# Reordering one seam of a gated-recurrence kernel: the third unit's scores, two output pieces, and ScalarE's copies of x

## The chip, the cores and the metric

The kernel runs on one core of a Trainium2 chip. Its time is the device time of one execution in microseconds (us); lower is better. The three runs of the kernel before gave 678.92, 680.96 and 681.97 us, so its median is 680.96 us.

## The reference

Two blocks follow each other. The first is a gated recurrence with a complex decay, over 4 batches, 8 heads, 768 positions and a head size of 48. Its output is read as 3072 tokens of width 384 and goes through a feed-forward block of width 2048 with an ELU.

```python
mag = sqrt(a_re**2 + a_im**2)
scale = minimum(mag, 0.999) / (mag + 1e-6)
a_re_n, a_im_n = a_re * scale, a_im * scale
for t in range(S):                       # S = 768
    S_re, S_im = (ar*S_re - ai*S_im + k_t v_t^T), (ar*S_im + ai*S_re)
    y[:, :, t] = q_t @ S_re
x = y.transpose(0, 2, 1, 3).reshape(B*S, H*D)
h = x @ w_in
g = where(h > 0, h, exp(minimum(h, 0)) - 1)
return g @ w_out
```

## The kernel before

**Units.** The work is cut into 12 units. A unit is 128 positions of two batches (so 256 tokens, GT), and the units of one pair of batches follow each other with a carried state. For every unit the kernel computes decays and angles (squares, logarithms, powers, lengths, ratios, slopes, angles, carried: ScalarE and VectorE), from them the gates (turns, waves, scaled, ends, gated), then on TensorE the transposes of the gated q and k, the scores, the products with v ("values") and with the carried states, and last the feed-forward block: eight times "inner" (two of 16 slices of w_in by x) with "elu" behind it, then the projection through w_out. TensorE is fed by every one of these.

**Order.** The program runs under a manual schedule: every engine and every DMA queue takes its instructions in the order in which the Python code emits them, and waits on semaphores that the tile framework puts in. For the first three units this order is a list written out by hand, `first` (L1429 to L1479); for the later ones it is a plan with slot numbers (L1489 to L1506). An entry such as `(project, 1, 0, 12, 16)` calls `project(u=1, n=0, f0=12, f1=16)`. The change lies in the last nine lines of this list, in which the projections of units 0 and 1 are spread as "pieces" between the steps of unit 2 (the third unit, `PAIRED` = 2) and the first steps of unit 3.

**A piece** is `project(u, n, f0, f1)` (L1205): four matmuls of 384 columns, written (u, n, f0, f1) below or, short, (u, n, f0). n is one half of the unit's tokens. The piece that ends at 16 also emits two ScalarE copies of 192 columns from PSUM to a tile `o` (L1224) and two output DMAs on SP's queue (L1225). The tag `o` has two buffers. The accumulators lie in PSUM: unit 0 has one bank of the tag `mlp` for each half; unit 1 has both halves in one tile of the tag `y`, which has one buffer:

```python
            if u == 0:
                x["o", n] = work([C, DM], "mlp")
            elif n == 0:
                t = ps.tile([C, NB, 512], FP32, tag="y", bufs=1, name="y")
                for m in range(NB):
                    x["o", m] = t[:, m, 0:DM]
```

PSUM's eight banks are three for `mlp`, three for `w` and two for `y`. `inner` (L1182) takes a bank of `mlp` for each call. When unit 2's inner begins, two of the three belong to the halves of unit 0's projection; the third was last used by `inner` (1, 14), whose elu comes much earlier in the list. Banks are given out in the order in which the program has given them back, so `inner` (2, 0) takes the third bank, (2, 2) that of the half n = 0 of unit 0 and (2, 4) that of n = 1; the later ones wait for the elus of these three.

**Around the third unit.** `states` (L1030) multiplies keys with values for the half 0 of unit 2. `transposed` (L1002) does eight TensorE transposes into two banks of `w`, and ScalarE copies each bank to SBUF (L1014). `scored` (L1116) does the state products of half 1 into two banks of `w` (L1054), then all scores into one tile `y` (L1126), and VectorE masks the two halves of it (L1134). `turns` of unit 3 is L832 on TensorE with four VectorE instructions behind it (L837, L840). `valued` (L1139) does the products with v into a new tile `y` (L1087), the sums of decays of unit 3 (`quartered`, L883), the products with the carried states (L1096), the exponentials of unit 3 on ScalarE (`quarters_used`, L898, and one DMA, L902), and last copies y to `x["x"]` and `x["y"]` on ScalarE (L1157, L1158). `seam` (L1162) moves rows of `x["y"]` to `x["x"]` by six DMAs, three on GpSimd's queue and three on SP's. `waves` of unit 3 is three ScalarE activations (L967, L970, L971). `convert` takes one step of rounding the weights, and does nothing once all of them are rounded: the list calls it 96 times for 80 steps, and the last step is taken before `(project, 1, 0, 4, 8)`.

Of the kernel before, what the change touches and what calls it, by code (L numbers as in the profile page):

```python
# [505 lines left out]
def kernel(  # L506
# [68 lines left out]
    nat = [{} for _ in range(NU)]  # L575
# [110 lines left out]
    def flat(t):  # L686
        return t.rearrange("p n h d -> p (n h d)")
# [5 lines left out]
    def new(tag, bufs=1, shape=None):  # L693
        return sb.tile(shape or [C, NB, H, D], FP32, tag=tag, bufs=bufs, name=tag)
# [182 lines left out]
    def quartered(u):  # L877

        x = nat[u]
        both = [work([C, HD]) for n in range(NB)]  # L880
        for c in range(C // L):
            for n, t in enumerate(both):
                nc.tensor.matmul(  # L883
                    t[ts(c ^ n, L)], lhsT=sum_logs[ts(c, L), ts(c, L)],
                    rhs=flat(x["l"][ts(c, L), n : n + 1]), start=True, stop=True,
                )
        return both

    def quarters_used(u, both):

        x = nat[u]
        for n, t in enumerate(both):
            for key, sign in (("E", 1.0), ("F", -1.0)):
                pairs = [(slice(0, C), slice(0, C))]
                if n:
                    pairs = [(ts(c, L), ts(1 - c, L)) for c in range(C // L)]
                for to, of in pairs:
                    nc.scalar.activation(  # L898
                        out=flat(x[key][to, n : n + 1]), in_=t[of], func=AF.Exp, scale=sign
                    )  # L900
        ends = dram.tile([NB, C // L, H, D], FP32, tag="ends", bufs=2, name="ends")
        nc.scalar.dma_start(  # L902
            out=ends.rearrange("n c h d -> c n (h d)"),
            in_=x["E"][L - 1 :: L].rearrange("p n h d -> p n (h d)"),
        )
        x["ends"] = ends
# [92 lines left out]
    PAIRED = 2  # L999
# [83 lines left out]
    def value_products(u, n, y, first=True):  # L1083
        x = nat[u]
        for p, c, j in EACH:

            nc.tensor.matmul(  # L1087
                y[ts(j, HP), c, ts(p, L)], lhsT=vn[u % 2][ts(c, L), n, ds((2 * p + j) * D, HP)],
                rhs=x["a", n][ts(c, L), 2 * p + j], start=(first and p == 0), stop=False,
                skip_group_check=True,  # L1090
            )
    def carried_products(u, n, y):
        x = nat[u]
        for p, c, j in EACH:
            if x["S", n][c] is not None:
                nc.tensor.matmul(  # L1096
                    y[ds(j * HP, D), c, ts(p, L)], lhsT=x["S", n][c][:, 2 * p + j],
                    rhs=x["qt", n][:, 2 * p + j, ts(c, L)], start=False, stop=False,
                    skip_group_check=True,
                )  # L1100
# [38 lines left out]
    def valued(u):  # L1139

        x = nat[u]
        y = ps.tile([C, C // L, 512], FP32, tag="y", bufs=1, name="y")
        for n in range(NB):
            value_products(u, n, y[:, :, ts(n, NP * L)], n == 0)
        if u + 1 < NU:
            both = quartered(u + 1)
        for n in range(NB):
            carried_products(u, n, y[:, :, ts(n, NP * L)])
        if u + 1 < NU:
            z = nat[u + 1]  # L1150
            z["E"], z["F"] = new("n", 6), new("n", 6)
            quarters_used(u + 1, both)
        x["x"], x["y"] = new("x", 2, [C, NI, GT]), new("y", 1, [C, GT])
        parts = y.rearrange("p c (n x t) -> p c n x t", n=NB, x=NP)
        to = x["x"].rearrange("p x (n c t) -> p c n x t", n=NB, c=C // L)
        for c in range(C // L):
            nc.scalar.copy(out=to[:, c], in_=parts[:, c, :, 0:NI])  # L1157
        nc.scalar.copy(  # L1158
            out=x["y"].rearrange("p (n c t) -> p c n t", n=NB, c=C // L), in_=parts[:, :, :, NI],
        )  # L1160
# [262 lines left out]
    def gates_of(u, *at):  # L1423
# [45 lines left out]
        *2 * [(convert,)], (project, 1, 1, 4, 8), (turns, 2), *2 * [(convert,)],  # L1469
        (project, 0, 1, 4, 8), (begun, 3), (squares, 3), *2 * [(convert,)],  # L1470
        (project, 1, 0, 8, 12), (waves, 2), (scaled, 2), (joined, 3), (gated, 2), (ends, 2),
        (load_qk, 3), (logarithms, 3), (powers, 3), (convert,), (project, 1, 1, 8, 12),
        *4 * [(convert,)], (states, 2, 0), *5 * [(convert,)], (project, 1, 0, 12, 16),
        (transposed, 2, "q", 0), (project, 1, 1, 12, 16), (transposed, 2, "k", 0), (lengths, 3),
        (ratios, 3), (slopes, 3), (transposed, 2, "q", 1), (angles, 3), (project, 0, 0, 8, 12),
        (transposed, 2, "k", 1), (carried, 3), (project, 0, 1, 8, 12), (scored, 2), (turns, 3),
        (project, 0, 0, 12, 16), (valued, 2), (seam, 2), (noted, 3), (waves, 3),
        (project, 0, 1, 12, 16), (scaled, 3), (ends, 3), (opened,),
    ]  # L1479
    def layer_of(u, at_h, at_p):  # L1480
        for m in range(NF // 2):
# [7 lines left out]
    for u in range(2, NU):  # L1489
        r = (u - 2) * SLOTS  # L1490
        put(r + (4 if u > PAIRED else 8), load_a, u)
        put(r + 8, load_v, u)
        put(r + 8, load_qk, u)
        if u == 2:
            decays_of(u, 16, 16, 17, 17, 18.4, 19.5, 19.6, 22.7, 19.8, 19.8)
            gates_of(u, 20.4, 21.6, 22.1, 22.4, 22.4, 22.6)
        else:
            decays_of(u, r + 7.2, r + 8.4, r + 12, r + 13.2, r + 13.4, r + 13.5, r + 14.9, r + 16.7, r + 15.5, r + 16.6)
            gates_of(u, r + 15, r + 18, r + 18.5, r + 18, r + 18, r + 19.5)
        if u > PAIRED:  # L1500
            for n in range(NB):
                put(r + 22 + 2 * n, transposed, u, "q", n)
                put(r + 23 + 2.3 * n, transposed, u, "k", n)
            put(r + 26.6, scored, u)
            put(r + (31 if u + 1 < NU else 29.3), valued, u)
            put(r + (31 if u + 1 < NU else 29.3), seam, u)  # L1506
        layer_of(u, range(r + 36, r + 44), range(r + 44, r + 52))
# [46 lines left out]
```

## Time and profile before

| | |
|---|---|
| median of three runs | 680.96 us |
| the profiled execution | 681.87 us |
| its span, first to last instruction | 680.1 us |
| TensorE busy (matmul) | 657.5 us, 97% |
| TensorE weight loads | 578.1 us, 85% |
| VectorE, ScalarE, GpSimd busy | 400.9, 395.9 and 184.2 us |
| granted TensorE clock, mean | 0.99 |
| the stage that the change reorders | 131.8 to 177.3 us of the span |

In the lists of the timeline a line gives the start in us, the duration, the engine (PE is TensorE, PEld its weight loads, DVE VectorE, ACT ScalarE, POOL GpSimd, SP the queue of SyncE), the line of the kernel, the operation, output and inputs with their shapes, the number of instructions, and in brackets how long the engine sat idle before it and what released it. Ends of matmuls are modelled, so two lines of PE may overlap by some tenths. One fp32 matmul of a piece shows as two instructions.

### The profile page before, as it was taken

Reading aid. Unit: us, or ns where it says so; the run is one execution under the profiler, and the core shown is the slowest. Engines: PE = TensorE matmul, PEld = TensorE weight load, DVE = VectorE, ACT = ScalarE, POOL = GpSimd, SP = SyncE. Lnnn points to the kernel's source line nnn. Section 1 sums busy time; section 2 is a strip of 40 time slices with the busy share of each in tenths; the row PEclk is TensorE's granted clock in tenths of the full one; section 3 lists DMA queues with packets and bytes.
Section 4 is the critical chain, followed back from the end, with each engine's and each line's share of the span. In section 5 each row is a group of like instructions: output and inputs, shape, how many; then the busy total and the mean of one; then the engine's idle time right before and its main releaser. Section 6 shows DMA issues by size and latency. Waiting matters only on the chain.

```text
span 680.1 us, 15754 instructions
## 1 busy us (share of the span) xinstructions
PE 657.5 (97%) x6656; PEld 578.1 (85%) x6656; DVE 400.9 (59%) x584; ACT 395.9 (58%) x620; POOL 184.2 (27%) x199
## 2 busy tenths in 40 slices
PE   8799898999999999999999999999999999999996
PEld 6777785566899899999999999999889889889995
DVE  5898999954775465465465465465564554642151
ACT  6875455875755755755756756657657557541230
POOL 2000000112114523433433433533434423501000
PEclk9799999999999999999999999999999999999999
DMA  9985744530902902812911821831821731200000
GB/s 169 187 141 93 146 144 167 109 71 20 166 12 68 149 26 66 140 37 62 142 39 54 134 54 54 134 56 54 125 64 53 137 53 52 50 2 7 24 1 29
DMA packets 149899, 55.98 MB, mean 82 GB/s; under 512 B 129172, under 2 KB 142652, under 8 KB 149820
## 3 DMA queue, kind: packets, MB, share of 16 engines
q1 hardware_dynamic: 146336, 53.57, 40.6%
q0 software_dynamic: 3264, 1.18, 1.7%
q8 instruction: 54, 0.88, 0.6%
q14 instruction: 25, 0.20, 0.1%
q10 hardware_dynamic: 220, 0.14, 0.1%
HBM read 48.88 MB, written 4.78 MB: 79 GB/s over the span
## 4 chain that ended last, share of the span: by engine, by line
PE 82%; DVE 9%; ACT 4%; issue 3%; DMA 1%; ACTq 0%; POOL 0%; DVEq 0%; POOLq 0%
PE mlp L1190 33%; PE mlp L1301 27%; PE w L1013 6%; PE y L1096 3%; PE y L1126 3%; PE w L1054 3%; PE y L1087 2%; PE w L832 2%; DVE wf L43 1%; DVE w_out L653 1%; DVE wp L50 1%; DVE g L1201 1%; PE mlp L1404 1%; PE y L1216 1%; PE w L883 1%
## 5 line engine op out<-in xcount | busy, mean ns | idle before, releaser
L1190 PE MATMUL mlp<-x,w_in 128*128 128x256 f32 x1152 | 262.6, 382 | 4.6 <-DVE g L1201 2.7
L1190 PEld LDWEIGHTS mlp<-x,w_in 128*128 128x128 f32 x1152 | 215.5, 191 | 34.8 <-DVE g L1201 3.1
L1199 ACT ACTIVATE ee<-mlp 128x512 f32<-128x512 f32 x96 | 57.3, 597 | 137.2 <-PE mlp L1190 128.3
L1201 DVE SCALAR_TENSOR_TENSOR g<-ee,mlp 128x512 f32<-128x512 f32 x96 | 65.6, 684 | 117.8 <-ACT ee L1200 107.9
L1301 PE MATMUL mlp<-w_out,g 128*128 128x192 f32 x640 | 110.3, 326 | 0.0
L1301 PEld LDWEIGHTS mlp<-w_out,g 128*128 128x128 f32 x640 | 105.5, 190 | 2.7
L1279 DVE TENSOR_TENSOR g<-g 128x512 f32<-128x512 f32 x80 | 67.4, 842 | 2.7
L1200 ACT ACTIVATE ee<-ee 128x512 f32<-128x512 f32 x96 | 60.5, 630 | 2.9
L1071 POOL TENSOR_TENSOR S<-S,T 128x384 f32<-128x384 f32 x36 | 29.9, 849 | 102.5 <-DVE S L1069 102.5
L1301 PE MATMUL mlp<-w,g 128*128 128x192 f32 x320 | 55.8, 329 | 0.0
L1301 PEld LDWEIGHTS mlp<-w,g 128*128 128x128 f32 x320 | 52.1, 190 | 0.6
L1170 POOL DMA_DIRECT2D x<-y x62 | 30.5, 498 | 75.1 <-ACT y L1158 38.0
L1320 ACT COPY o<-mlp 128x192 f32<-128x192 f32 x10 | 3.2, 319 | 67.8 <-DMA out_dram<-o 39.9
L898 ACT ACTIVATE n<-w 64x384 f32<-64x384 f32 (+1 forms) x60 | 28.1, 486 | 18.4 <-PE w L883 17.7
L993 POOL TENSOR_TENSOR kg<-k,cs 128x1536 f32<-128x1536 f32 x8 | 34.8, 4351 | 12.6 <-issue 12.5
L856 POOL DMA_DIRECT2D carry<-n x10 | 5.1, 505 | 120.0 <-DVE n L840 120.0
L716 POOL TENSOR_TENSOR n<-n 128x768 f32<-128x768 f32 x8 | 16.5, 2059 | 67.6 <-ACT n L710 67.6
L759 POOL TENSOR_TENSOR n<-ar,n 128x768 f32<-128x768 f32 x8 | 14.9, 1861 | 61.0 <-ACT n L747 61.0
L1301 PE MATMUL mlp<-wt,g 128*128 128x192 f32 x160 | 29.4, 327 | 0.0
L1013 PE MATMUL w<-ident,qg 128*128 128x128 f32 x192 | 26.3, 283 | 1.9 <-ACT kt L1014 1.2
L993 DVE TENSOR_TENSOR qg<-q,cs 128x1536 f32<-128x1536 f32 (+1 forms) x12 | 19.5, 1622 | 14.8 <-ACT cs L971 14.8
L821 DVE SCALAR_TENSOR_TENSOR n<-carry,n 1x768 f32<-1x768 f32 x10 | 9.5, 947 | 31.5 <-ACT n L815 31.5
(173 smaller groups left out, 1008.8 us busy)
## 6 DMA issues: line engine op xcount, KB each, us to landing
w<-in_moe_w_out_dram SPq DMA_DIRECT2D x8, 768.0 KB
g<-in_moe_w_in_dram SPq DMA_DIRECT2D x16, 384.0 KB
g<-in_moe_w_out_dram SPq DMA_DIRECT2D x16, 384.0 KB
w<-in_moe_w_in_dram SPq DMA_DIRECT2D x16, 288.0 KB
vn<-in_v_dram SPq DMA_DIRECT2D x24, 192.0 KB
out_dram<-o SPq DMA_DIRECT2D x48, 96.0 KB
ar<-in_a_re_dram SPq DMA_DIRECT2D x22, 192.0 KB
ai<-in_a_im_dram SPq DMA_DIRECT2D x22, 192.0 KB
```

What stands on the lines that cost most here:

```text
L898: nc.scalar.activation(out=flat(x[key][to, n : n + 1]), in_=t[of], func=AF.Exp, scale=sign)
L993: eng.tensor_tensor(out=to[:, :, :, 0:D], in0=each.unsqueeze(2).to_broadcast([C, step * H, 2, D]), in1=x["cs"][:, n * H : (n + step) * H], ...
L1013: nc.tensor.transpose(t[:, h], of, ident)
L1054: nc.tensor.matmul(to, lhsT=of, rhs=vn[u % 2][ts(c, L), n, ts(h, D)], start=True, stop=True,)
L1071: eng.tensor_tensor(out=new_s, in0=new_s, in1=wide, op=ALU.mult)
L1170: eng.dma_start(out=x["x"][ds(j * HP + D, G), i], in_=x["y"][ds(j * HP + i * G, G)])
L1190: nc.tensor.matmul(t[:, e], lhsT=w_in[:, i, ts(f + e, C)], rhs=x["x"][:, i], start=(i == 0), stop=(i == NI - 1),)
L1199: nc.scalar.activation(out=e, in_=t, func=AF.Relu, scale=-1.0)
L1200: nc.scalar.activation(out=e, in_=e, func=AF.Exp, scale=-1.0)
L1201: nc.vector.scalar_tensor_tensor(out=x["g", f // 8][:, f % 8 : f % 8 + 2], in0=e, scalar=-1.0, in1=t, op0=ALU.add, op1=ALU.max)
L1279: nc.vector.tensor_tensor(out=S_of(u, k, h), in0=a, in1=b, op=op)
L1301: nc.tensor.matmul(to, lhsT=a[:, m], rhs=b[:, m], start=(first and h == 0 and m == 0), stop=False, skip_group_check=True,)
```

## The change

In `valued`, the three copies of y become a function of their own, `copied`. For unit 2 it is called before the exponentials of unit 3, for the later units after them, as before. In the list, the calls of the last part are put in another order, and ten calls of `convert`, all of them empty, are taken out.

```diff
@@ def valued(u)
+        if u == PAIRED:
+            copied(u, y)
         if u + 1 < NU:
             z = nat[u + 1]
             z["E"], z["F"] = new("n", 6), new("n", 6)
             quarters_used(u + 1, both)
+        if u > PAIRED:
+            copied(u, y)
+
+    def copied(u, y):
+        x = nat[u]
         x["x"], x["y"] = new("x", 2, [C, NI, GT]), new("y", 1, [C, GT])
...
@@ first = [
-        (load_qk, 3), (logarithms, 3), (powers, 3), (convert,), (project, 1, 1, 8, 12),
-        *4 * [(convert,)], (states, 2, 0), *5 * [(convert,)], (project, 1, 0, 12, 16),
-        (transposed, 2, "q", 0), (project, 1, 1, 12, 16), (transposed, 2, "k", 0), (lengths, 3),
-        (ratios, 3), (slopes, 3), (transposed, 2, "q", 1), (angles, 3), (project, 0, 0, 8, 12),
-        (transposed, 2, "k", 1), (carried, 3), (project, 0, 1, 8, 12), (scored, 2), (turns, 3),
-        (project, 0, 0, 12, 16), (valued, 2), (seam, 2), (noted, 3), (waves, 3),
-        (project, 0, 1, 12, 16), (scaled, 3), (ends, 3), (opened,),
+        (load_qk, 3), (logarithms, 3), (powers, 3), (project, 1, 0, 12, 16),
+        (states, 2, 0), (project, 1, 1, 8, 12), (transposed, 2, "q", 0), (lengths, 3),
+        (ratios, 3), (project, 0, 0, 8, 12), (transposed, 2, "k", 0), (transposed, 2, "q", 1),
+        (slopes, 3), (angles, 3), (project, 1, 1, 12, 16), (transposed, 2, "k", 1),
+        (carried, 3), (scored, 2), (turns, 3), (project, 0, 1, 8, 12), (valued, 2), (seam, 2),
+        (noted, 3), (waves, 3), (project, 0, 0, 12, 16), (scaled, 3), (ends, 3),
+        (project, 0, 1, 12, 16), (opened,),
```

## The prediction, made before the run

> **What bounds the kernel now.** I read the page first: TensorE is busy for 97% of the span and is 82% of the chain that ended last, so only TensorE's gaps can be won, and any new gap is lost in full.
>
> ```profile
> span 680.1 us, 15754 instructions
> ...
> PE 657.5 (97%) x6656; PEld 578.1 (85%) x6656; DVE 400.9 (59%) x584; ACT 395.9 (58%) x620; POOL 184.2 (27%) x199
> ...
> PE 82%; DVE 9%; ACT 4%; issue 3%; DMA 1%; ACTq 0%; POOL 0%; DVEq 0%; POOLq 0%
> ```
>
> Then TensorE's waits in the stretch that the change reorders (100 to 190 us; columns: us in total, times, longest). The first lies before the change.
>
> ```profile
> PE mlp L1216 <- DVE g L1201: 1.8, 1, 1.8
> PE mlp L1190 <- DMA x<-y: 1.6, 1, 1.6
> PE w L1013 <- ACT kt L1014: 1.2, 1, 1.2
> PE w L1054 <- DVE kg L993: 0.2, 1, 0.2
> ```
>
> So two waits can be won here, 1.6 us for x and 1.2 us for a `w` bank, under 3 us of 681. From 180 us to the end the same view shows one TensorE wait of 0.4 us: later stages absorb nothing. A delay here is a delay of the end.
>
> Last the timeline. The reader is to see which ScalarE line stands ahead of which TensorE line.
>
> ```profile
> 137.34 1.15 PE L1054 MATMUL w<-vn,kg 64*64 64x48 f32 x64 [0.18 <-DVE kg L993]
> ...
> 138.41 2.85 PE L1216 MATMUL y<-w_out,g 128*128 128x384 f32 x8
> ...
> 140.53 0.83 ACT L747 ACTIVATE n<-n 128x768 f32<-128x768 f32 x1
> ...
> 141.30 0.54 ACT L1224 COPY o<-y 128x192 f32<-128x192 f32 x2
> ...
> 141.97 2.77 PE L1216 MATMUL y<-w_out,g 128*128 128x384 f32 x8
> ...
> 146.16 0.56 ACT L1224 COPY o<-y 128x192 f32<-128x192 f32 x2 [3.34 <-PE w L1013]
> ...
> 147.26 0.66 PE L1013 MATMUL w<-ident,qg 128*128 128x128 f32 x4 [1.22 <-ACT kt L1014]
> ...
> 154.97 1.15 PE L1126 MATMUL y<-qt,kt 128*64 128x64 f32 x32
> ...
> 157.10 0.69 DVE L1134 TENSOR_TENSOR a<-y,mask 128x512 f32<-128x512 f32 x1 [1.47 <-PE y L1126]
> ...
> 162.79 1.99 PE L1096 MATMUL y<-qt,S 128*48 128x64 f32 x64
> ...
> 165.95 0.86 ACT L1157 COPY x<-y 128x384 f32<-128x384 f32 x2
> 166.69 0.39 ACT L1158 COPY y<-y 128x256 f32<-128x256 f32 x1
> ...
> 169.13 8.34 PE L1190 MATMUL mlp<-x,w_in 128*128 128x256 f32 x36 [1.57 <-DMA x<-y]
> ...
> 170.00 0.94 ACT L971 ACTIVATE cs<-cs,quarter 128x768 f32<-128x768 f32 x1
> 170.85 0.52 ACT L1224 COPY o<-mlp 128x192 f32<-128x192 f32 x2
> ```
>
> The wait at 147.26 is not k's transposes: ScalarE's copies of k stood behind the copies of (1,1,12), at 146.16. TensorE had ended that piece by 144.74, so these waited for something else, and what is left is their `o` buffer, still being written out.
>
> [...] The halves of unit 1's `y` tile, 512 fp32 each, are two banks, [...] whether the program's semaphores do is another question. The mask of half 0 says they don't: at 157.10 it began behind the scores of both halves, although those of half 0 took from 154.97 to 156.12. [...] Here, with an idle queue, an output DMA issued at 217.97 released a ScalarE copy at 219.72: 1.75 us, which I use.
>
> **The change part by part.** TensorE's work is the same, so I add up its gaps. From start to start, without a wait: a piece 2.60 (141.97 to 144.57), eight transposes 0.87, state products 1.08, scores 2.01, turns 1.40, values 0.98, quartered 0.76, carried products 1.92, an inner 2.72 (8.17 for three).
>
> *The empty converts:* nothing is emitted for them; cost 0.
>
> *(1,0,12) ahead of the states.* TensorE ends it at 137.15 and the states at 138.49, as before. But its two copies stay behind powers of unit 3 on ScalarE, which is busy without a gap up to L747's end at 141.36: they run at 141.3 to 141.84, as before. The next piece, (1,1,8), writes the same tile `y`. If the tile is guarded as a whole, as the mask suggests, it must wait for both copies and starts at about 141.92 instead of 138.41: **a new gap of 3.5 us**, and everything behind it on TensorE queues. Before, (1,1,12) had the same neighbour and started at 141.97, right after these copies, so the wait was covered by q's transposes. From both sides: 0 if the halves are apart, 3.5 if not; I take 3.5.
>
> *Transposes and the other pieces.* From 141.92: q0 at 144.52, (0,0,8) 145.4, k0 148.0, q1 148.9, (1,1,12) 149.8, k1 152.4, end of its dense slot 153.25. The copies of k0 now find ScalarE free and the `o` copies are far away, so **the gap at 147.26 goes: -1.4** (the transposes would have been due at 145.89). ScalarE then has q1's copies to 150.6, the table load and arctan of angles (2.17 from 148.67 to 150.84) to 152.8, copies of (1,1,12) to 153.3, and k1's first copy to 153.85. The state products of `scored` need that bank: they start at about 153.9 instead of 153.25, **a new gap of 0.65**. The scores follow at 154.98; the `y` tile was free at 153.3. That is where they stood before (154.97), one piece poorer: (0,0,12) now comes later. Turns, masks and VectorE's chain keep their times; (0,1,8) takes the slot of (0,0,12). The carried products again stand at 162.8 to 164.8.
>
> *Copies of x ahead of the exponentials, two pieces behind.* The copies run at 164.9 to 166.05 instead of 165.95 to 167.08; x is complete 2.8 us after that (before: 167.08 to the weight load at 169.86), at 168.9. The pieces (0,0,12) and (0,1,12) fill TensorE to 169.9. `inner` (2,0) starts there without a wait: **the gap at 169.13 goes: -1.8** (its due time was 164.71 + 2.60 = 167.31). SP and GpSimd have nothing ahead of the seam's DMAs but the carry's, issued at 161.45. The cover is 1.0 us.
>
> *What ScalarE then owes.* Exponentials with their load and DMA issue take 4.16 (161.76 to 165.92) and end at 170.2; waves takes 3.84 (167.10 to 170.94) and ends at 174.05. Only then come the copies of (0,0,12), 173.95 to 174.5. Before, they ran at 161.2. `inner` (2,2) needs their bank; it is due at 172.65 and starts at 174.55: **a new gap of 1.9**. It could be 0 only if another bank were given, which the order of the releases excludes.
>
> *Then (0,1,12)'s copies.* They want the `o` buffers just filled: 174.3 + 1.75 = 176.05, and the second at 176.4 to 176.7. `inner` (2,4) is due at 177.27, so this is hidden, with 0.5 us to spare. elu (2,0) behind it ends at 179.95 (relu, load, exp and VectorE took 3.27 from 172.32); `inner` (2,6) is due at 180.9, behind transposes. Unit 3's exponentials end 4.3 us later than before, but its gated q by 177.6, and its transposes are due at 180.0: covered. The loads of v and a on SP, now behind the last output pieces, start some 5 us later, with 10 us before TensorE asks for v.
>
> *Sum:* 3.5 + 0.65 + 1.9 - 1.4 - 1.8 = **+2.85**; followed start by start, the transposes of unit 3 come at 180.0 instead of 177.3: **+2.7**, which I take. On the profiled execution 681.87 + 2.7 = 684.6; that execution lies 0.9 above the median, so on the median **683.7 us**, 0.4% longer. I reckon 0.5% as about the least that a measurement of this kernel tells from no change (3.4 us): I forecast a small loss, just within it.
>
> **The rivals.**
>
> *A, the halves of `y` are guarded apart.* For it: they lie in two banks; against it: the mask at 157.10. Without the 3.5, TensorE runs ahead, angles holds the state products a little longer (0.8 instead of 0.65), and the scores come at 151.65, 3.3 earlier: 683.7 - 3.3 = 680.4. No change.
>
> *B, ScalarE also serves (0,0,12)'s bank in time* (and A holds): -1.9 more, 678.5. It needs waves and exponentials hidden, which their measured durations speak against.
>
> *C, slower: the second pair of output copies blocks ScalarE.* Its price is the landing of an output DMA. Between the copies at 141.3 and 146.16 it was 3.2 us from the issue at 142.94, with loads of q and k in the queues. From 0.5 us above my 1.75 it decides: at 3.2, `inner` (2,4) waits 1.0 us more, and each further 1 us, or a late elu (2,0), comes on top: 683.7 + 1.0 = 684.7, to 686. For it: elus, copies and loads queue behind one wait. Against it: the loads now come after these DMAs, so the queue is idle.
>
> **How the numbers follow.** Forecast 0.58, C 0.2, A 0.12, B and anything better 0.1. The likeliest case's own range, with 0.2% of spread between runs, is 682.3 to 685.3. To leave out no more than 2 in 10 the range takes in most of C and of A: 680.0 to 686.0. Slower by over 0.5% (above 684.4): most of C and a quarter of the forecast, 0.35. Faster by over 0.5% (below 677.6): 0.05, the far side of B. Within: 0.60.
>
> **What would show it.** In the profile after: TensorE's wait for ACT L1224 of 3.5 us ahead of an L1216 on `y` near 138.5; one of 0.6 ahead of L1054; none for x at `inner` (2,0); one of 1.9 for L1224 ahead of L1190. No L1216 wait would mean A; a further one ahead of the third inner, C. I am wrong in kind if unit 3's transposes start before 177.3.

## The result, and the profile after

The changed kernel takes **685.52 us** (median of six runs, 684.57 to 687.31) against 681.07 us for the kernel before (six runs beside them, 678.92 to 681.97): a ratio of 1.0068, with a 95% interval of 1.0049 to 1.0086, or 4.5 us more. (The ratios are worked out from all the runs and differ a little from those of the medians. Each is against the kernel before, measured beside it; times taken at different occasions are best compared through them.) The time lies inside the predicted range, 1.8 us above the predicted 683.7, and just beyond the 0.5% that I had put down as "no change".

The page of the kernel after, its profiled execution being one of 684.57 us:

```profile
span 682.8 us, 15757 instructions
...
PE 657.2 (96%) x6656; PEld 577.8 (85%) x6656; DVE 400.7 (59%) x584; ACT 395.6 (58%) x620; POOL 184.0 (27%) x199
...
PE 80%; DVE 8%; ACT 4%; SPq 3%; DMA 2%; issue 2%; ACTq 0%; DVEq 0%
```

No engine has more work than before. TensorE's share of the chain fell from 82 to 80%, and the part of the span in which it is not busy rose from 22.6 to 25.6 us. TensorE's waits of the stage in the kernel after (128 to 190 us; us in total, times, longest; the change moved L1190, L1216 and L1224 to L1197, L1223 and L1231):

```profile
PE y L1223 <- ACT o L1231: 3.4, 1, 3.4
PE mlp L1197 <- ACT o L1231: 1.8, 1, 1.8
PE w L1054 <- ACT cs L1014: 0.2, 1, 0.2
PE w L1054 <- DVE kg L993: 0.2, 1, 0.2
```

The two waits of before, for x and for k's bank, are gone. Two new ones stand in their place, both for copies to `o`. The timeline of the kernel after shows where:

```profile
129.31 5.32 PE L1223 MATMUL y<-w_out,g 128*128 128x384 f32 x16
...
138.00 0.83 ACT L747 ACTIVATE n<-n 128x768 f32<-128x768 f32 x1
...
138.73 0.52 ACT L1231 COPY o<-y 128x192 f32<-128x192 f32 x2
...
139.30 4.52 PE L1223 MATMUL y<-w_out,g 128*128 128x384 f32 x8 [3.35 <-ACT o L1231]
...
143.66 1.04 PE L1013 MATMUL w<-ident,qg 128*128 128x128 f32 x8
...
152.92 1.14 PE L1054 MATMUL w<-vn,kg 64*64 64x48 f32 x60 [0.18 <-ACT cs L1014]
...
163.73 5.43 PE L1223 MATMUL mlp<-w_out,g 128*128 128x384 f32 x16
...
163.85 0.86 ACT L1164 COPY x<-y 128x384 f32<-128x384 f32 x2 [10.49 <-PE y L1096]
...
169.00 2.75 PE L1197 MATMUL mlp<-x,w_in 128*128 128x256 f32 x12
...
172.93 0.52 ACT L1231 COPY o<-mlp 128x192 f32<-128x192 f32 x2
...
173.50 5.45 PE L1197 MATMUL mlp<-x,w_in 128*128 128x256 f32 x24 [1.75 <-ACT o L1231]
...
175.49 0.54 ACT L1231 COPY o<-mlp 128x192 f32<-128x192 f32 x2 [2.04 <-DMA out_dram<-o]
...
178.79 1.04 PE L1013 MATMUL w<-ident,qg 128*128 128x128 f32 x8
```

Read the line at 139.30 twice. Its bracket is the wait I had forecast. Its duration is not: the same eight instructions took 2.85 us before, now 4.52. The windows of the same trace tell why (stretch, us, busy time of PE, PEld, DVE, ACT and POOL with instructions, granted clock, DMA share, GB/s): the gap, the 3.4 us behind it, and the 3.4 us after those:

```profile
136.00:139.30 3.30, 0.00 (x0) 0.00 (x0) 2.35 (x5) 3.24 (x5) 1.66 (x2) 1.00 0.57 114
139.30:142.70 3.40, 3.40 (x6) 1.88 (x7) 3.33 (x3) 0.00 (x0) 0.64 (x1) 0.50 1.02 180
142.70:146.10 3.40, 3.40 (x17) 2.34 (x16) 0.04 (x1) 1.07 (x2) 0.00 (x0) 1.00 0.02 4
```

Right behind the gap TensorE is granted half its clock (0.50), for one stretch of 3.41 us.

Below, **the stage** is the time from the start of the two `y` pieces ahead of the state products (129.31 here) to the first transposes of unit 3 (178.79 here): 45.47 us before, 49.48 after, +4.0. I compare stages rather than spans because the stage begins between 129.3 and 135.4 us in the profiles of this study: the half-clock stretches ahead of it, where no kernel here alters anything, differ in place and number (before, from 21.42 to 28.25 us and from 48.73 to 52.14; after, one, from 19.82 to 26.65). A stage is that of a single profiled execution; the times are medians of many. The profile after happened to start its stage 2.5 us earlier than that of before, so its span shows too little of the loss.

### The profile page after: what moved, and what is told of

Same layout as the page of the kernel before. It is cut to its first block, busy times and chain, and to the rows that moved or that the text cites. A ratio compares the mean times of both kernels' runs of the same rounds, so it can differ in the third digit from the quotient of the medians.

```text
span 682.8 us, 15757 instructions
## 1 busy us (share of the span) xinstructions
PE 657.2 (96%) x6656; PEld 577.8 (85%) x6656; DVE 400.7 (59%) x584; ACT 395.6 (58%) x620; POOL 184.0 (27%) x199
## 4 chain that ended last, share of the span: by engine, by line
PE 80%; DVE 8%; ACT 4%; SPq 3%; DMA 2%; issue 2%; ACTq 0%; DVEq 0%
PE mlp L1197 33%; PE mlp L1308 27%; PE w L1013 5%; PE y L1126 3%; PE y L1096 3%; PE w L1054 3%; SPq L596 2%; PE w L832 2%; PE y L1087 2%; DVE wf L43 1%; DMA w<-in_moe_w_in_dram 1%; DMA w<-in_a_im_dram 1%; PE w L883 1%; PE y L1223 1%; PE mlp L1223 1%
## 5 line engine op out<-in xcount | busy, mean ns | idle before, releaser
L1197 PE MATMUL mlp<-x,w_in 128*128 128x256 f32 x1152 | 260.8, 380 | 4.8 <-DVE g L1208 2.7
L1197 PEld LDWEIGHTS mlp<-x,w_in 128*128 128x128 f32 x1152 | 214.3, 190 | 34.5 <-DVE g L1208 3.1
L1014 ACT COPY qt<-w 128x512 f32<-128x512 f32 x48 | 25.4, 582 | 8.0 <-PE w L1013 8.0
```

Of the source, the lines that this page charges most:

```text
L1014: nc.scalar.copy(out=o[:, h0 : h0 + 4], in_=t)
L1197: nc.tensor.matmul(t[:, e], lhsT=w_in[:, i, ts(f + e, C)], rhs=x["x"][:, i], start=(i == 0), stop=(i == NI - 1),)
```

## The experiments

My theory: the loss is the two waits for ScalarE plus a half-clock stretch that the longer one brings. The rivals: the slow piece is slowed by the loads of q and k that run beside it (180 GB/s in the second window); or the early copies of x, not the pieces, are what costs.

**1. The copies of (1,0,12) ahead of unit 3's logarithms.** All of the change is kept; on ScalarE alone the two `o` copies pass a queue of activations.

```diff
-(load_qk, 3), (logarithms, 3), (powers, 3), (project, 1, 0, 12, 16),
+(load_qk, 3), (project, 1, 0, 12, 16), (logarithms, 3), (powers, 3),
```

> The changed kernel with the piece (1,0,12) listed ahead of the logarithms of unit 3. TensorE's order is the same, since the logarithms and powers are ScalarE's; only the two output copies of that piece move ahead of five ScalarE instructions and two table loads. Theory (TensorE waits for copies queued behind ScalarE's powers, and then runs at half clock because it idled): the wait of 3.4 us and the slow piece behind it both go, the stage from the first of the two y pieces to unit 3's transposes falls from 49.5 to about 44.6 us, and the time to about 680.6 us, level with the kernel before; logarithms start some 2 us later, which is covered. Rival (the piece is slow because the loads of q and k run at the same time, whatever TensorE did before): the wait goes but the piece keeps its 4 us or so, stage 46, time 682. Second rival (the wait is TensorE's order, not ScalarE's): no change, 685.5.

681.32 us, ratio 0.9993 (0.9977 to 1.0009): the whole loss is gone; the stage is 44.36. Its timeline:

```profile
140.76 0.54 ACT L1231 COPY o<-y 128x192 f32<-128x192 f32 x2 [1.74 <-PE y L1223]
...
141.95 2.85 PE L1223 MATMUL y<-w_out,g 128*128 128x384 f32 x8
```

The copies run as soon as the piece is done, the next piece in the tile `y` starts without a wait and takes 2.85 us again. The second wait stays (1.75 us). So the first gap, with what it brings, is worth 5.1 us of stage (49.48 - 44.36), not the 3.35 that it lasts.

**2. The exponentials back ahead of the copies of x**, with the new list.

```diff
-        if u == PAIRED:
-            copied(u, y)
...
-        if u > PAIRED:
-            copied(u, y)
+        copied(u, y)
```

> The changed kernel with the copies of x behind the exponentials of unit 3 again, as before; the new list stays. Theory: with two output pieces behind the values the copies need no priority; the exponentials go back under the carried products, ScalarE is through with waves some 3 us earlier, and the wait of 1.75 us for the bank of the first output half goes. x comes about 1.1 us later, which the second piece still covers to within some tenths. Expected 1.5 us below the changed kernel, 684.0. Rival (the early copies are what saved the wait for x): a wait for x of about 1 us returns ahead of the first inner, the bank is then free, and the time falls by only 0.7 us.

685.08 us, 1.0048 (1.0032 to 1.0065); stage 48.85. Its timeline:

```profile
141.38 5.49 PE L1220 MATMUL y<-w_out,g 128*128 128x384 f32 x8 [3.35 <-ACT o L1228]
...
165.39 2.38 ACT L898 ACTIVATE n<-w 128x384 f32<-128x384 f32 x5 [7.27 <-PE w L883]
...
168.28 0.86 ACT L1161 COPY x<-y 128x384 f32<-128x384 f32 x2
...
172.46 7.93 PE L1194 MATMUL mlp<-x,w_in 128*128 128x256 f32 x36
...
173.18 0.52 ACT L1228 COPY o<-mlp 128x192 f32<-128x192 f32 x2
```

The second wait is gone: the three inners run in one block from 172.46, as the copies to `o` now come at 173.18, in time for the second one. ScalarE has the same work ahead of these copies as in the kernel after, but the exponentials no longer stand behind the copies of x, which wait for the carried products: they start 34.0 us into the stage instead of 37.0. And x is not late, though copied behind the exponentials: the two pieces (5.3 us) cover it. The time is some 1.5 us below that of the changed kernel by the ratios (1.0048 against 1.0068 and 1.0071), as expected. Against the first profile of the changed kernel the stage shows only 0.6 us of it, since in this profile two half-clock stretches (6.83 us) came with the first gap, and the piece took 5.49 us.

**3. The early copies of x alone**, with the list of before.

```diff
+        if u == PAIRED:
+            copied(u, y)
         if u + 1 < NU:
...
+        if u > PAIRED:
+            copied(u, y)
```

> The kernel before with only the early copies of x; its list is as before, with one piece behind the values. Theory: the copies run 1.1 us earlier, so the wait for x of 1.57 us ahead of the first inner shrinks to about 0.5; the exponentials end later, but the only bank they hold up is that of the second half, 5 us from its use: 680.0, 1 us below the kernel before. Rival (the exponentials that no longer lie under the carried products hold up elu and the gates of unit 3): no gain, or a wait for a gate ahead of unit 3's transposes, 681 to 682.

682.84 us, 1.0009 (0.9987 to 1.003); stage 45.48, nothing won or lost. The timeline:

```profile
167.54 5.69 PE L1197 MATMUL mlp<-x,w_in 128*128 128x256 f32 x24 [0.47 <-DMA x<-y]
...
173.42 0.52 ACT L1231 COPY o<-mlp 128x192 f32<-128x192 f32 x2
...
173.99 2.86 PE L1197 MATMUL mlp<-x,w_in 128*128 128x256 f32 x12 [0.77 <-ACT o L1231]
```

The wait for x fell from 1.57 to 0.47 us, and the third inner got a new one of 0.77 for its bank: the exponentials, now behind the copies of x, push waves, and waves the copies to `o`. The gain is given back in the same stage. I had expected 1 us less, with that bank 5 us away from its use: this was wrong.

**4. Twelve matmuls in the gap.** Matmuls with the identity, of no use for the result, before the piece that waits (`warm`, whose lines are left out here; the trace shows 24 instructions).

```diff
-(states, 2, 0), (project, 1, 1, 8, 12),
+(states, 2, 0), (warm, 12), (project, 1, 1, 8, 12),
```

> The changed kernel with twelve matmuls of the identity, of no use to the result, between the states of unit 2 and the piece (1,1,8), that is in the gap in which TensorE waits for the output copies (about 2.8 us of work in 3.4 us). Theory [...]: the gap is as long as before but no longer idle, the clock stays at 1.0, the piece takes 2.8 us instead of 4.5, and the time falls by 1.5 us to 684.0. Rival (the loads of q and k slow the piece): no effect, or up to 0.5 us slower; the piece still takes 4.5 us at a granted clock of 1.0.

Its windows, the former gap and the piece behind it:

```profile
138.00:141.20 3.20, 2.72 (x24) 2.53 (x24) 2.25 (x5) 3.14 (x5) 1.66 (x2) 1.00 0.42 83
141.20:143.90 2.70, 2.70 (x9) 1.59 (x10) 2.63 (x3) 0.00 (x0) 0.64 (x1) 1.00 1.17 223
```

The clock stays at 1.00 and the piece takes 2.85 us, with *more* traffic beside it (223 GB/s) than in the slow piece (180). That refutes the loads as the cause: with TensorE busy in the gap (2.72 of 3.20 us), the clock did not fall. But the time did not fall: 686.93 us, 1.0074 (1.0047 to 1.0102), stage 49.22. What took the place of the won time is in the timeline:

```profile
175.54 0.32 ACT L1231 COPY o<-mlp 128x192 f32<-128x192 f32 x1 [1.86 <-DMA out_dram<-o]
...
177.37 0.32 ACT L1231 COPY o<-mlp 128x192 f32<-128x192 f32 x1 [1.51 <-DMA out_dram<-o]
...
177.74 2.86 PE L1197 MATMUL mlp<-x,w_in 128*128 128x256 f32 x12 [1.14 <-ACT o L1231]
```

The first of the two `o` buffers came free as in the kernel after (1.86 against 2.04 us of waiting), the second 1.5 us after it, and the third inner waited 1.14 us. This is the mechanism of my rival C. Up to the first inner the kernel keeps what the clock gave back: this starts 38.02 us into the stage (169.23 - 131.21), in the kernel after 39.69 (169.00 - 129.31), so 1.67 us are won, the price of one half-clock stretch. Behind it the late buffer takes most of them again.

The packets in the trace show what ran while the second output was held back. Of its 128 packets, 120 had started by 175.3; the last eight started from 176.20 on, one after another. In between, one packet of 16 KB on the queue that the profile calls "instruction" ran, from 174.86 to 176.21. The DMA queues from 174.8 to 176.2 (packets, MB, share of 16 engines' time):

```profile
q1 hardware_dynamic: 136, 0.09, 21.4%
q8 instruction: 1, 0.02, 6.1%
```

6.1% of 16 engines for 1.4 us is about 1.37 us of one engine, and while this packet ran, the output's last eight packets did not start. In the kernel after, no packet of this queue runs between 163.0 and 177.5.

Against the kernel before, the time is that of the changed kernel (1.0074 against 1.0068 and 1.0071, with overlapping intervals), though the stage is a little shorter. The rest of this profile is longer: 505.6 us from the stage's end to the end of the span, against 504.0 in the kernel after and 502.8 before. Behind 190 us TensorE has one wait of 0.4 us before, and here four:

```profile
PE y L1126 <- issue: 1.8, 4, 0.6
```

For "issue" the profile shows nothing that was waited for. But each of these four waits ends 1.4 to 1.5 us after a packet of the instruction queue has arrived, and so do, after 1.3 to 1.6 us, all the others of this kind in the profiles of this study. That the added instructions make TensorE run short of instructions there is my reading; no run tests it.

**5. Copies to `o` ahead of waves.** Everything of the change is kept, the copies of (0,0,12) go ahead of waves on ScalarE.

```diff
-(noted, 3), (waves, 3), (project, 0, 0, 12, 16), (scaled, 3),
+(noted, 3), (project, 0, 0, 12, 16), (waves, 3), (scaled, 3),
```

> The changed kernel with the piece (0,0,12) listed ahead of waves of unit 3: TensorE's order is the same, but its two output copies stand ahead of the three ScalarE activations of waves and their table load. Theory (the bank of the second inner is held up by ScalarE's order): the wait of 1.75 us ahead of the second inner goes, and the output buffers have landed when the other half's copies want them; waves ends 0.5 us later, so the gated q is ready just when unit 3's transposes are due, and up to 0.3 us is given back. Stage 48.0 us with the slow piece still in it; time 684.0. Rival (the wait moves on): a wait of more than 1 us for VectorE's gated q or for the third inner's bank takes its place, time 685 to 685.5.

684.49 us, 1.0038 (1.0021 to 1.0054), stage 47.68. TensorE's waits of the stage:

```profile
PE y L1223 <- ACT o L1231: 3.4, 1, 3.4
PE w L1054 <- DVE kg L993: 0.2, 1, 0.2
PE w L1054 <- ACT cs L1014: 0.2, 1, 0.2
PE w L1013 <- DVE qg L993: 0.2, 1, 0.2
```

The second wait is gone, and only 0.17 us for a gated q has come in its place: 1.8 us of stage are won, about as long as the wait lasted. The first gap is there, with one half-clock stretch.

**6. Two pieces swapped**, (1,0,12) back behind the states.

```diff
-(powers, 3), (project, 1, 0, 12, 16), (states, 2, 0), (project, 1, 1, 8, 12),
+(powers, 3), (project, 1, 1, 8, 12), (states, 2, 0), (project, 1, 0, 12, 16),
```

> The changed kernel with its first move undone: (1,1,8) ahead of the states of unit 2 and (1,0,12) behind them, as before; the rest of the new order stays. Theory (the wait comes from the tile y being guarded whole while its copies stand behind ScalarE's powers): TensorE reaches (1,0,12) when ScalarE is nearly free, no piece that writes y follows it closely, so the wait of 3.4 us and the low clock go as in the first experiment; the wait of 1.75 us for the output bank stays. Stage 44.4 us, time 681.0. Rival (any order in which a piece writes y after those copies waits): a wait of 1 us or more for L1231 stays ahead of a piece on y, time 682 to 684.

681.26 us, 0.9985 (0.9971 to 0.9998), stage 44.40, the clock at 1.00. The waits:

```profile
PE mlp L1197 <- ACT o L1231: 1.8, 1, 1.8
PE w L1054 <- DVE kg L993: 0.2, 1, 0.2
PE w L1054 <- ACT cs L1014: 0.2, 1, 0.2
```

No wait on `y` is left, and the second wait is as in the kernel after. A different edit, in TensorE's order, gives the same stage as experiment 1 (44.36). In the order of before, the piece into the same tile does not stand right behind the one whose copies are blocked.

**7. Experiments 2 and 4 together**, twice, since the first time did not fit its stage.

```diff
-        if u == PAIRED:
-            copied(u, y)
...
-(states, 2, 0), (project, 1, 1, 8, 12),
+(states, 2, 0), (warm, 12), (project, 1, 1, 8, 12),
```

> The changed kernel with the copies of x behind the exponentials, as in the second experiment, and twelve matmuls of the identity in the gap ahead of (1,1,8). In the second experiment's profile the granted clock was 0.5 for 6.8 us behind the gap, two windows, in the changed kernel's for 3.4 us, and here no output copies stand in TensorE's way later. Theory (an idle TensorE loses its clock): the clock stays at 1.0, the stage falls from 48.9 to about 46.0 us, the time to 682.0. Rival (the gap costs the same whatever fills it, since the piece is slowed by loads, or filling it delays what is behind): stage 47.5 or more, 684 to 685.

> The kernel with the exponentials first and the filled gap once more: its stage in the profile was 0.35 us longer than before, its time by the ratio 1.8 us longer, which do not fit. If that was chance, the time comes out within 0.2% of the kernel before. If the filled gap doesn't always hold the clock, the second profile shows half clock behind it, or a late output buffer as in the fourth experiment, and the ratio stays near 1.0026.

Stages 45.82 and 46.44 against 48.85 of experiment 2, the clock at 1.00 behind the filled gap in both; 1.0026 (1.0012 to 1.004) and 1.0019 (1.0001 to 1.0037) against 1.0048. The second profile has 0.36 us of a late `o` buffer again, and again a 16 KB packet of the instruction queue (172.34 to 174.04) ahead of the last packets of an output. The stage falls by 2.4 to 3.0 us, about what the half clock had cost in experiment 2 (3.1 us, below), but the time by only 1.5 to 2.0. The stages are 0.35 and 0.97 us longer than before, the times 1.8 and 1.3 us by the ratios (intervals 0.8 to 2.7 and 0.1 to 2.5 us).

In these profiles too the difference lies behind the stage: 505.1 and 504.7 us are left from its end, 2.3 and 1.9 more than before. Waits ahead of L1126 like those of experiment 4, four and three of them, take 1.9 and 1.6 us in total against 0.4; the rest I can't place.

**8. Experiments 1 and 2 together**, and **the changed kernel again**, without an edit.

```diff
-        if u == PAIRED:
-            copied(u, y)
...
-(load_qk, 3), (logarithms, 3), (powers, 3), (project, 1, 0, 12, 16),
+(load_qk, 3), (project, 1, 0, 12, 16), (logarithms, 3), (powers, 3),
```

> The new list with (1,0,12) ahead of the logarithms of unit 3, and the copies of x behind the exponentials: both costs of the change are taken out, its two gains stay. Theory: no wait for output copies is left on TensorE, x is covered by the two pieces; stage 42.7 us against 45.5 before, time 678.5, 2.7 us below the kernel before. Rival (the two waits covered others): a new wait of a microsecond or more turns up for x, the gates of unit 3 or an output buffer, time 680 to 681, no better than before.

> The changed kernel once more, for a second profile beside the runs of this call. Theory: the wait for the output copies is again 3.4 us, and one or two windows of half clock follow it; stage 49.5 us or, with two windows, 51. Rival (the low clock of the first profile was chance): the gap is there, the clock stays at 1.0 behind it, and the stage is 48.0.

Both waits out: 679.86 us, 0.9965 (0.9949 to 0.9981), stage 43.08, now 2.4 us below that of before. The changed kernel again: 1.0071 (1.005 to 1.0093), stage 50.31. Its windows, from the end of the gap to the transposes:

```profile
142.20:147.30 5.10, 5.08 (x8) 2.72 (x9) 3.38 (x3) 0.00 (x0) 0.65 (x1) 0.51 0.73 125
```

This time two half-clock stretches (6.83 us in all) came with the same gap of 3.36 us, and from the piece to the next instruction it is 5.16 us (142.22 to 147.38) instead of 4.36. They did not begin at the end of the gap, but in it, as the windows of the gap show:

```profile
138.86:140.42 1.56, 0.00 (x1) 0.00 (x0) 0.94 (x2) 1.55 (x2) 0.54 (x1) 1.00 0.00 0
140.42:142.22 1.80, 0.00 (x1) 0.01 (x1) 1.48 (x3) 1.74 (x4) 1.13 (x2) 0.50 1.03 205
```

In the four profiles with this gap half clock cost half of the time that TensorE worked under it. From the gap's end to the end of half clock it was 3.40 us in the first profile of the changed kernel, 5.03 here, 3.12 in experiment 5 and 6.21 in experiment 2. Half of each is 1.7, 2.5, 1.6 and 3.1 us; the work behind the gap took 1.76, 2.56, 1.61 and 3.14 us longer than at full clock. So what the gap brings varies from execution to execution with the time at which half clock sets in and the number of its stretches.

**9. Experiments 6 and 2 together:** the pieces swapped, the exponentials ahead of the copies of x; what is left of the change is the order of the transposes and scores with the pieces between them, and the two pieces behind the values.

```diff
-        if u == PAIRED:
-            copied(u, y)
...
-(powers, 3), (project, 1, 0, 12, 16), (states, 2, 0), (project, 1, 1, 8, 12),
+(powers, 3), (project, 1, 1, 8, 12), (states, 2, 0), (project, 1, 0, 12, 16),
```

> The new list with (1,1,8) and (1,0,12) in the old places and the copies of x behind the exponentials. Theory: like the version with both costs taken out, but the logarithms of unit 3 don't have to stand behind the output copies; no wait over 0.3 us on TensorE in the stage, stage 42.8 us, time 2.7 us below the kernel before. Rival: as fast as that version at best, since x is the next late thing (0.2 us there): 2.4 us below.

**678.68 us, 0.9944 (0.9926 to 0.9961)**: faster than both kernels, 3.3 us below the median of the kernel before beside it (681.97), 3.8 by the ratio. The stage is 42.37. TensorE's waits of the stage, the whole list:

```profile
PE w L1054 <- ACT cs L1014: 0.2, 1, 0.2
PE w L1054 <- DVE kg L993: 0.2, 1, 0.2
```

and of its timeline:

```profile
137.79 2.85 PE L1220 MATMUL y<-w_out,g 128*128 128x384 f32 x8
...
140.67 0.54 ACT L1228 COPY o<-y 128x192 f32<-128x192 f32 x2
...
165.82 7.93 PE L1194 MATMUL mlp<-x,w_in 128*128 128x256 f32 x36
...
173.59 1.04 PE L1013 MATMUL w<-ident,qg 128*128 128x128 f32 x8
```

The copies to `o` run no earlier against the stage's start than in the kernel after (9.45 us behind it, there 9.42): nobody waits for them, since the next piece on TensorE goes to another accumulator.

The stages beside the times, each against the kernel before:

| kernel | stage, us | ratio |
|---|---|---|
| changed, two measurements | +4.0, +4.8 | 1.0068, 1.0071 |
| 1 copies ahead | -1.1 | 0.9993 |
| 2 exponentials first | +3.4 | 1.0048 |
| 3 only the copies of x | 0.0 | 1.0009 |
| 4 gap filled | +3.8 | 1.0074 |
| 5 `o` ahead of waves | +2.2 | 1.0038 |
| 6 pieces swapped | -1.1 | 0.9985 |
| 7 is 2 with 4, twice | +0.4, +1.0 | 1.0026, 1.0019 |
| 8 is 1 with 2 | -2.4 | 0.9965 |
| 9 is 6 with 2 | -3.1 | 0.9944 |

## Why the prediction was nearly right, and where it fell short

**The piece behind (1,0,12).** I took the tile `y` to be guarded as a whole and the gap to be 3.5 us; it is 3.35. Experiments 1 and 6 take it away in two ways. Rival A, the halves guarded apart, falls; whether they could be was not tried. This step carries the sign of the result.

**The state products.** 0.65 us forecast; they start at 152.43 and 152.92 where 152.4 was due (143.66 and the 8.7 us of my steps), so some 0.5 is lost.

**The gaps won.** Both went, as forecast: no wait for x at the first inner and none for k's bank. But experiment 2 shows that the pieces alone do the first of these. The early copies of x gain nothing beside them and cost the second wait.

**The bank of the second inner.** 1.9 us forecast, 1.75 measured; experiment 2 removes it by letting the exponentials start earlier, experiment 5 by putting the copies ahead of waves.

**The copies of (0,1,12).** They waited 2.04 us for their `o` buffers and were hidden, as forecast. Rival C's place was right as well, but in the changed kernel it did not decide. In experiment 4 it did, there with a packet of the instruction queue ahead of an output's last packets, a term that the prediction did not have.

**The term that was too small: "a new gap of 3.5 us, and everything behind it on TensorE queues".** I priced the gap at its length and put the clock behind it at nothing. There it was half: the piece and its successor are 4.36 us apart instead of 2.60, +1.76, and 5.16 in the second profile, +2.56. With the sizes as measured, my sum is 3.35 + 0.5 + 1.75 - 1.4 - 1.8 = 2.4; with the clock 4.2 and 5.0, against measured stages of +4.0 and +4.8. The forecast's mechanism was right and this one cost was missing. "Within 0.5%", my likeliest outcome, was lost by just that: without the 1.76 to 2.56 us of the clock, 685.52 would be 683.0 to 683.8. That the time still lies inside the range is in part luck: the range reached up to 686.0 for the sake of rival C, which had no part in it.

The traces show this of the clock. The half-clock stretches behind the gap take 3.41 us (the first profile of the changed kernel, experiment 5; the expectations call this a window) or 6.83 us (the second, experiment 2). Half clock set in when TensorE had idled for 3.34, 3.06, 1.56 and 2.73 us in these four profiles, and gaps of 1.75 us elsewhere in the stage left the clock at 1.00. All four profiles with the gap of 3.35 us show half clock; none of the stage's gaps of 1.8 us and less does.

**Open:** the cause of the waits behind the stage in experiments 4 and 7, where the coincidence with the instruction queue is seen but not tested; and what decides whether and when half clock sets in. The stage has no gap between 1.8 and 3.35 us. Ahead of it, in the profile before, a gap of 2.66 us (up to 77.76) left the clock at 1.00, while half clock set in at 48.73 with no wait over 0.27 us in the 4.9 us before.

## What to carry to other kernels

When an accumulator tile is split in two halves but tracked as one, put work for another accumulator between the last piece of one half and the first of the next, or let the copies out go ahead of long ScalarE work: here either is worth about 5 us of the stage, the half clock included. Price a gap of TensorE like this one (3.35 us) at its length plus half of the time that TensorE works at half clock behind it (1.6 to 3.1 us more here), and where it can't be removed, judge filling it by the time, since the filled kernels didn't get all of it back. Of a change that moves several things at once, try the halves apart: two of its parts here gain 3.3 us and the other two lose more than that.

## What I had not expected of the hardware

The same idle gap (3.35 and 3.36 us) cost 1.76 us of half clock in one profile and 2.56 in another of the same kernel: one stretch set in at the gap's end, two stretches 1.8 us ahead of it. And two output DMAs, issued one behind the other, released their `o` buffers nearly together in the changed kernel (both copies from 175.49 to 176.03), but 1.5 us or more apart in experiment 4 (ScalarE's copies at 175.54 and 177.37) and in the second run of experiment 7 (173.42 and 175.20). In both of these the last eight packets of an output started only as a 16 KB packet of the instruction queue ended (1.36 and 1.69 us long), and so it is in the first run of experiment 7, where nobody waited for it. No run moves this packet; the coincidence in three profiles is all that speaks for it.
